# Reading x back in small packets and turning it on VectorE in a fused attention and FFN kernel

## The chip, the core and the metric

The kernel runs on one core of a Trainium2 chip. The time is device microseconds of one launch, the median of three runs; a profiled execution of the same program gives the trace. TensorE is the matrix engine, VectorE and ScalarE work on rows of up to 128 partitions, GpSimd (POOL) takes some elementwise work, and SP issues nearly all DMAs.

## The reference

Attention of 8 heads over 8 batches of 576 tokens, the first four heads local (each token sees the 32 up to itself), the last four strided (each sees the earlier ones at the same place modulo 32); then a layer norm, a two-layer FFN and the residual, all in float32:

```python
scores = scale * np.matmul(q, k.transpose(0, 1, 3, 2))        # q, k, v: (8, 8, 576, 64)
scores = np.where(masks, scores, -1e9)                        # local for h < 4, else strided
attn = softmax(scores)
x = np.matmul(attn, v).transpose(0, 2, 1, 3).reshape(8, 576, 512)
xn = (x - mean(x)) / sqrt(var(x) + 1e-6) * g_ln
out = x + np.maximum(xn @ w_ch1, 0.0) @ w_ch2                 # 512 -> 2048 -> 512
```

## The kernel before

**The FFN** runs in nine chunks of 512 tokens: chunk c below 8 is the first 512 tokens of batch c, chunk 8 the last 64 of all batches. A chunk has 16 steps, one for each 128 columns of the hidden layer. In a step, `ffn1` (L708 and L715) multiplies the step's part of w_ch1 by x, whose features stand on the partitions, into one PSUM tile `ph`; `h_high` (L720, ScalarE) and `h_low` (L725, VectorE) take the relu out of it in a high and a low part; `second` (L735) then does the second matrix for the step before. Each product is three matmuls with high and low parts, so x is needed as `xh` and `xl`, both with features on partitions and tokens on columns. The layer norm is folded in: w_ch1 is centred and scaled beforehand, and the row's scale is applied at the end (`finish`, L741) together with the residual. `ph` has a single buffer, so the next step's L708 waits for L720 and L725.

**The attention** of a batch is four pairs of heads, `Pair`, strided and local in turn. Batches 0 and 1, all weights and chunk 0 are ordered by hand in `ORDER`. From chunk 1 on the pairs of the batch behind the chunk's own are spread over the steps: the generator `pieces` (L893) takes one pair in four steps, called at L923 behind a step's relu and ahead of `second`. So chunks 1 to 6 hold the 24 pairs of batches 2 to 7. A pair is done as follows, `nxt` being the pair behind it:

- Step one, `m_piece`: TensorE makes the scores of `nxt` (L443) and the products of this pair with v (L514) in a PSUM tile; VectorE sums, masks and divides (L534 to L564) into `xo`; `v_store` (L576, L577 or L581) writes `xo` to a scratch tensor in DRAM, `xdl` for local pairs in the order of the tokens, `xds` for strided ones with the 32 residues outermost. Then the loads of v for two pairs on (L392, L393, L399).
- Step two: VectorE turns the raw q and k of the third pair on in 32x32 blocks (L413, L414, L418), and SP loads those of the fourth on (L349), 32 partitions by 18 groups of 128 bytes a DMA, eight DMAs. The raw tile has one buffer.
- Step three, `n_piece`: TensorE turns `xo` in 128x128 tiles (`x_turns`, L586; 4 for a local pair, 6 for a strided one) and the softmax numerators of `nxt` (`p_turn`, L499; 5 or 6), into one PSUM tile; ScalarE copies x out as `xh` (L613), VectorE subtracts for `xl` (L617), and ScalarE copies the turned numerators to `pt` (L504).
- Step four: nothing.

Near the end of a chunk, `x_load` (L671, L673) reads its rows of x back from the scratch for the residual, into tiles of the pool `tkp` (seven buffers), and `x_scale` (L678 to L683) takes their statistics; `finish` stores the output (L744, in the last chunk L747 as well).

The order of every engine's instructions, SP's included, is that of the program: a closing loop chains each instruction to the one before it on its engine. An instruction that waits holds up what stands behind it on its engine.

Of the kernel before, what the change touches and what calls it, by code (L numbers as in the profile page):

```python
# [8 lines left out]
F32 = mybir.dt.float32  # L9
# [55 lines left out]
def kernel(  # L65
# [10 lines left out]
    nc = tc.nc  # L76
# [3 lines left out]
    P = 128  # L80
    STR = 32
    NB = S // STR
    NG = (STR + 2) // 3
    GS = 3 * NB
    D1 = D + 1
    NL = (NB + 3) // 4
    NS = (NG + 1) // 2
    NCC = DM // P
    NFC = DFF // P
    CH = 512  # L90
# [10 lines left out]
    tkp = ctx.enter_context(tc.tile_pool(name="tkp", bufs=7))  # L101
# [31 lines left out]
    for jj in range(4):  # L133
        mrow = mask_l[STR * jj:STR * (jj + 1)]
        nc.gpsimd.affine_select(
            out=mrow, in_=mrow, pattern=[[1, 64]], base=-1,
            channel_multiplier=-1, compare_op=ALU.is_ge, fill=FILL)
        nc.gpsimd.affine_select(
            out=mrow, in_=mrow, pattern=[[-1, 64]], base=STR,
# [5 lines left out]
    for c in range(2):  # L145
        for r in range(3):
            msk = mask_s[64 * c:64 * (c + 1), NB * r:NB * (r + 1)]
            nc.gpsimd.affine_select(
                out=msk, in_=msk, pattern=[[-1, NB]], base=-NB * r,
                channel_multiplier=1, compare_op=ALU.is_ge, fill=FILL)  # L150
            nc.gpsimd.affine_select(
                out=msk, in_=msk, pattern=[[0, NB]], base=NB * r + NB - 1,
# [56 lines left out]
    xd_l = [dram.tile([S, DM // 2], F32, name=f"xdl{b}") for b in range(B)]  # L209
    xd_s = [dram.tile([2 * NS * GS, DM // 2], F32, name=f"xds{b}") for b in range(B)]  # L210
# [93 lines left out]
    def bank(name):  # L304
        pool, tag, n = banks[n_bank[0] % len(banks)]
        n_bank[0] += 1
        return pool.tile([P, n], F32, tag=tag, name=name)
# [11 lines left out]
    class Pair:  # L319
# [180 lines left out]

        def p_copy(self, pp):
            pool, tag = (early, f"pt{self.k % 2}") if self.b == 0 else (smp, "pt")
            self.pt = pool.tile([P, NS, P], F32, tag=tag, name=f"pt{self.id}")
            nc.scalar.copy(  # L504
                out=self.pt[:, 0:self.nt].rearrange("p t x -> p (t x)"), in_=pp[:, 0:P * self.nt])

        def v_block(self, n, h, at, w):
            if self.local:
                t, jj = divmod(n, 4)
                rows, cols = slice(64 * h, 64 * h + 64), slice(STR * jj, STR * (jj + 1))  # L510
            else:
                t, c = divmod(n, 2)
                rows, cols = slice(64 * h, 64 * h + GS), slice(64 * c, 64 * c + 64)
            nc.tensor.matmul(  # L514
                at(h, t)[cols], self.pt[rows, t, cols], self.v[rows, n, 0:w],
                start=True, stop=True, tile_position=(64 * h, cols.start))

        def v_full(self, ps):
            self.av = halves(ps, self.nt, D1)
# [36 lines left out]
        def v_divide(self, parts):  # L556
            nt = self.nt
            den = dens[self.i_den]
            if self.b == 0:
                xo = early.tile([P, NS, 2, D], F32, name=f"xo{self.id}")  # L560
            else:
                xo = xo_c
            for r, h0, h1, t0, t1, av in parts:
                nc.vector.tensor_tensor(  # L564
                    out=xo[r, t0:t1, h0:h1].rearrange("p t h d -> p h t d"), in0=av,
                    in1=den[r, h0:h1, t0:t1].unsqueeze(3).broadcast_to(
                        [r.stop, h1 - h0, t1 - t0, D]),
                    op=ALU.mult)
            self.xov = xo.rearrange("p t h d -> p t (h d)")

        def v_store(self):
            n0, nt, xov = self.n0, self.nt, self.xov
            cs = slice(P * n0, P * (n0 + 1))
            if self.local:
                x_b = xd_l[self.b]
                nc.sync.dma_start(x_b[0:CH, cs].rearrange("(t p) c -> p t c", p=P), xov[:, 0:NT])  # L576
                nc.sync.dma_start(x_b[CH:S, cs], xov[0:REST, NT])  # L577
            else:
                x_b = xd_s[self.b].rearrange("(t c s) d -> c s t d", c=2, s=GS)
                for c in range(2):  # L580
                    nc.sync.dma_start(x_b[c, :, :, cs], xov[64 * c:64 * c + GS, 0:nt])  # L581

        def x_turns(self, px):
            nt = NT if self.local else NS
            for t in range(nt):
                nc.tensor.transpose(px[:, P * t:P * (t + 1)], self.xov[:, t], ident)  # L586
            return nt
# [32 lines left out]
    def m_piece(p, nxt):  # L620

        ps = bank(f"m{p.id}")
        parts = nxt.s_blocks(ps) if nxt else None
        p.v_sums()
        av = p.v_blocks(ps)
        if nxt:
            nxt.s_masked(parts)
        p.v_divide(av)
        p.v_store()
        if nxt:  # L630
            nxt.s_sub()
            nxt.s_exp()

    def n_piece(p, nxt):

        ps = bank(f"n{p.id}")
        n = P * p.x_turns(ps)
        if nxt:
            nxt.p_turn(ps[:, n:])
        p.x_high(ps)  # L640
        p.x_low()
        if nxt:
            nxt.p_copy(ps[:, n:])

    def split_x(hi, lo, src):
        nc.scalar.activation(out=hi, in_=src, func=AF.Copy)
        nc.vector.tensor_tensor(out=lo, in0=src, in1=hi.bitcast(F32), op=ALU.subtract)
# [3 lines left out]
    def x_t(c):  # L651
        if c not in xt:
            xt[c] = tuple(xtp.tile([P, NCC, CH], F32R, tag=t, name=f"{t}{c}")
                          for t in ("xh", "xl"))
        return xt[c]
# [4 lines left out]
    pairs = [Pair(b, hp) for b in range(B) for hp in order]  # L660
# [62 lines left out]
    def h_low(c, f, ph, hh):  # L723
        hl = hp_.tile([P, CH], F32R, tag="hl", name=f"hl{c}_{f}")
        nc.vector.scalar_tensor_tensor(  # L725
            out=hl, in0=ph, scalar=0.0, in1=hh.bitcast(F32), op0=ALU.max, op1=ALU.subtract)
        return hl
# [53 lines left out]
    ps, ph, hs, splits = {}, {}, {}, {}  # L781
# [111 lines left out]
    def pieces():  # L893
        for i in range(2 * NHP, NP):
            nxt = pairs[i + 1] if i + 1 < NP else None
            m_piece(pairs[i], nxt)
            if i + 2 < NP:
                pairs[i + 2].load_v()
            yield
            if i + 3 < NP:  # L900
                pairs[i + 3].t_piece()
            if i + 4 < NP:
                pairs[i + 4].load_qk()
            yield
            n_piece(pairs[i], nxt)
            yield
            yield

    gen = pieces()
    ps_r_ctx.close()  # L910
    ps_m = ctx.enter_context(tc.tile_pool(name="ps_m", bufs=1, space=bass.MemoryType.PSUM))
    banks[:] = [(ps_m, "m", 1536)]

    for c in range(1, NCHUNK):
        xres = []
        tail = {}
        for f in range(NFC):
            ph = ffn1(c, f)
            hh = h_high(c, f, ph)
            h = hh, h_low(c, f, ph, hh)  # L920
# [3 lines left out]
            elif c + 1 == B:  # L924
                i = f // 2 - 1
# [6 lines left out]
            i = f - (NFC - NT - 3)  # L932
# [49 lines left out]
```

## Time and profile before

| | us |
|---|---|
| median of 3 runs (933.94 to 936.65) | 936.09 |
| the profiled execution | 935.35 |
| its span, first to last instruction | 933.5 |
| TensorE matmuls busy (7852) | 915.0 |
| TensorE weight loads busy, beside the matmuls | 756.8 |
| VectorE busy | 407.2 |
| ScalarE busy | 222.6 |
| GpSimd busy | 148.1 |

The mean granted clock of TensorE over the span is 0.992 of full speed. Matmul records overlap, as the next one starts before the end of the one before; where the time per instruction matters, it is read from the distance of starts in the timeline. The trace of DMAs has their issue on SP and the share of the span in which the 16 DMA engines are busy, but no landing of a single DMA.

### The profile page before, as it was taken

What the parts mean: (1) busy time and instruction counts of PE and PEld (TensorE: products, weight loads), DVE (VectorE), ACT (ScalarE), POOL (GpSimd) and SP (SyncE); (2) the same over time, 40 slices, a digit from 0 to 9 for tenths busy, and PEclk for the clock granted to TensorE, in tenths of its full rate; (3) what the DMA queues carried; (4) which work ended last, traced back from release to release, by engine and by line L of the source; (5) the groups of instructions that cost most, each with busy time, mean ns of one, the idle gap of its engine ahead of it and who ended that gap; (6) DMA issues with size and microseconds to landing.
All of it is one profiled execution on the core that took longest, in us unless ns stands there. A gap on an engine that the chain in (4) does not pass through costs nothing.

```text
span 933.5 us, 18590 instructions
## 1 busy us (share of the span) xinstructions
PE 915.0 (98%) x7852; PEld 756.8 (81%) x7852; DVE 407.2 (44%) x829; ACT 222.6 (24%) x361; POOL 148.1 (16%) x186
## 2 busy tenths in 40 slices
PE   8699999999999999999999999999999999999997
PEld 7578888888888888888888888888888888888886
DVE  3878877333444454435443454334533321122112
ACT  4567662112111211111121211121211111111110
POOL 5568773000100010001000110001000000000000
PEclk9799999999999999999999999999999999999999
DMA  8987966333443344324342334334221130002001
GB/s 154 231 248 188 270 145 126 94 57 87 75 98 65 86 75 98 64 55 90 76 79 46 82 60 99 64 87 75 73 38 49 37 108 17 1 1 90 1 1 46
DMA packets 239459, 80.16 MB, mean 86 GB/s; under 512 B 190096, under 2 KB 232720, under 8 KB 239376
## 3 DMA queue, kind: packets, MB, share of 16 engines
q1 hardware_dynamic: 236672, 77.27, 36.3%
q10 hardware_dynamic: 2704, 1.70, 0.8%
q8 instruction: 62, 1.02, 0.5%
q14 instruction: 21, 0.17, 0.1%
HBM read 59.48 MB, written 19.46 MB: 85 GB/s over the span
## 4 chain that ended last, share of the span: by engine, by line
PE 89%; SPq 4%; DMA 3%; DVE 1%; issue 1%; POOL 0%; ACT 0%; DVEq 0%; ACTq 0%
PE po L735 40%; PE ph L708 26%; PE ph L715 13%; SPq L349 3%; PE m L514 2%; PE m L443 2%; PE n L499 1%; PE n L586 1%; DMA s<-in_moe_w_ch_dram 1%; PE t L369 1%; DMA rows<-in_q_dram 1%; DMA xds<-xo 1%; SPq L399 1%; PE s L443 1%; PE av L514 0%
## 5 line engine op out<-in xcount | busy, mean ns | idle before, releaser
L735 PE MATMUL po<-w,hh 128*128 128x512 f32 x1152 | 361.5, 395 | 0.0
L725 DVE SCALAR_TENSOR_TENSOR hl<-ph,hh 128x512 fp32r<-128x512 f32 x144 | 99.6, 692 | 459.7 <-ACT hh L720 459.2
L735 PEld LDWEIGHTS po<-w,hh 128*128 128x128 f32 x1152 | 211.7, 188 | 43.6
L708 PE MATMUL ph<-xh,w 128*128 128x512 f32 x576 | 225.9, 392 | 1.1 <-ACT w L292 0.9
L735 PE MATMUL po<-w,hl 128*128 128x512 f32 x576 | 225.0, 391 | 0.0
L708 PE MATMUL ph<-xl,w 128*128 128x512 f32 x576 | 224.3, 389 | 0.0
L720 ACT ACTIVATE hh<-ph 128x512 fp32r<-128x512 f32 x144 | 86.1, 598 | 500.7 <-PE ph L715 500.7
L715 PE MATMUL ph<-xh,w 128*128 128x512 f32 x576 | 154.6, 390 | 0.0
L708 PEld LDWEIGHTS ph<-xh,w 128*128 128x128 f32 x576 | 108.3, 188 | 23.8 <-ACT w L292 1.1
L735 PEld LDWEIGHTS po<-w,hl 128*128 128x128 f32 x576 | 108.1, 188 | 23.2
L708 PEld LDWEIGHTS ph<-xl,w 128*128 128x128 f32 x576 | 108.3, 188 | 22.0
L715 PEld LDWEIGHTS ph<-xh,w 128*128 128x128 f32 x576 | 107.7, 188 | 22.3
L489 POOL TENSOR_TENSOR sm<-sm,mx 128x648 f32<-128x648 f32 (+1 forms) x32 | 40.7, 1271 | 404.4 <-DVE mx L484 404.4
L683 POOL TENSOR_TENSOR rs<-rs,mhalf 128x1 f32<-128x1 f32 x36 | 19.8, 550 | 340.3 <-DVE rs L682 340.3
L495 ACT ACTIVATE sm<-sm 128x648 f32<-128x648 f32 (+1 forms) x32 | 23.8, 744 | 118.1 <-POOL sm L489 118.1
L296 POOL TENSOR_TENSOR w<-r,w 128x512 fp32r<-128x512 f32 x32 | 41.0, 1297 | 9.1 <-ACT w L292 8.7
L617 DVE TENSOR_TENSOR xl<-n,xh 128x480 fp32r<-128x480 f32 (+2 forms) x36 | 22.7, 662 | 15.5 <-ACT xh L613 15.5
L484 DVE TENSOR_REDUCE mx<-sm 128x12 f32<-128x648 f32 (+1 forms) x32 | 26.3, 823 | 2.1
L564 DVE TENSOR_TENSOR xo<-m,den 64x64 f32<-64x64 f32 (+3 forms) x120 | 27.1, 290 | 0.1
L741 DVE SCALAR_TENSOR_TENSOR x<-po,rs,x 128x512 f32<-128x512 f32 x36 | 24.5, 739 | 3.1 <-PE po L735 2.8
L678 DVE BATCH_NORM_STATS2 st<-x 128x6 f32<-128x512 f32 x36 | 24.3, 675 | 0.0
L613 ACT ACTIVATE xh<-n 128x480 fp32r<-128x480 f32 (+2 forms) x36 | 20.7, 649 | 11.3 <-PE n L499 11.3
(98 smaller groups left out, 611.0 us busy)
## 6 DMA issues: line engine op xcount, KB each, us to landing
s<-in_moe_w_ch_dram SPq DMA_DIRECT2D x32, 512.0 KB
out_dram<-x SPq DMA_DIRECT2D x32, 256.0 KB
raw<-in_q_dram SPq DMA_DIRECT2D x112, 72.0 KB
raw<-in_k_dram SPq DMA_DIRECT2D x112, 72.0 KB
xds<-xo SPq DMA_DIRECT2D x32, 162.0 KB
v_l<-in_v_dram SPq DMA_DIRECT2D x32, 144.0 KB
xdl<-xo SPq DMA_DIRECT2D x16, 256.0 KB
x<-xdl SPq DMA_DIRECT2D x32, 128.0 KB
```

The lines of the kernel that those rows point to most:

```text
L296: nc.gpsimd.tensor_tensor(out=t[:, 1], in0=self.w[i], in1=t[:, 0].bitcast(F32), op=ALU.subtract)
L349: nc.sync.dma_start(self.raw[p0:p0 + 32, i].rearrange("p (g e) -> p g e", e=32), src[self.b, self.h0 + h].rearrange("(g t) d -> t g d", t=32)[
L443: nc.tensor.matmul(o, lhsT, rhs, start=True, stop=True, tile_position=(64 * h, pos))
L484: nc.vector.reduce_max(mx[:, :, 0:nt], sm, axis=AX.X)
L489: nc.gpsimd.tensor_tensor(out=sm, in0=sm, in1=mx[:, :, 0:nt].unsqueeze(3).broadcast_to([P, 2, nt, sm.shape[3]]), op=ALU.subtract)
L564: nc.vector.tensor_tensor(out=xo[r, t0:t1, h0:h1].rearrange("p t h d -> p h t d"), in0=av, in1=den[r, h0:h1, t0:t1].unsqueeze(3).broadcast_to(
L708: nc.tensor.matmul(ph, w1h[:, cc], x[:, cc, :], start=(new and n == 0 and i == 0), stop=False)
L715: nc.tensor.matmul(ph, w1l[:, cc], xt[c][0][:, cc, :], start=False, stop=(cc == NCC - 1))
L720: nc.scalar.activation(out=hh, in_=ph, func=AF.Relu)
L725: nc.vector.scalar_tensor_tensor(out=hl, in0=ph, scalar=0.0, in1=hh.bitcast(F32), op0=ALU.max, op1=ALU.subtract)
L735: nc.tensor.matmul(po[i], hx[:, cs], w, start=(f == 0 and n == 0), stop=(f == NFC - 1 and n == 2))
L741: nc.vector.scalar_tensor_tensor(out=x, in0=po[i], scalar=rs, in1=x, op0=ALU.mult, op1=ALU.add)
```

## The change

For the 24 pairs of `pieces`, x is no longer turned by TensorE out of `xo`. Right behind the store, `x_raw` reads the pair's 512 tokens of 128 features back from the scratch with four DMAs, each for 32 features: token t of a group of 32 goes to partition t, so every packet is 32 floats, 128 bytes, at a row pitch of 1 KB in DRAM. In step three `x_blocks` turns that tile in 32x32 blocks on VectorE, into the space of `xo`, which the store has left by then, and splits the result into `xh` and `xl` by one ScalarE copy and one VectorE subtraction (`split_x`), for both kinds of pairs. The numerators of the next pair are turned by TensorE as before, in a PSUM tile of their own, and copied to `pt` ahead of the split. Batches 0 and 1 are as before.

```diff
+        def x_raw(self):
+            self.xraw = tkp.tile([P, CH], F32, tag="tk", name=f"xraw{self.id}")
+            x_b = (xd_l if self.local else xd_s)[self.b]
+            for j in range(4):
+                c0 = P * self.n0 + 32 * j
+                cols = x_b[:, c0:c0 + 32]
+                src = (cols[0:CH].rearrange("(g t) e -> t g e", t=32) if self.local else
+                       cols[0:STR * NB].rearrange("(t g) e -> t g e", g=NB)[:, 0:CH // 32, :])
+                nc.sync.dma_start(
+                    self.xraw[32 * j:32 * j + 32].rearrange("p (g e) -> p g e", e=32), src)
+
+        def x_blocks(self):
+            xh, xl = x_t(self.b)
+            cc = self.h0 // 2
+            xT = self.xo.rearrange("p t h d -> p (t h d)")[:, 0:CH]
+            nc.vector.transpose(xT, self.xraw)
+            split_x(xh[:, cc, :], xl[:, cc, :], xT)
...
-    def n_piece(p, nxt):
-
-        ps = bank(f"n{p.id}")
-        n = P * p.x_turns(ps)
-        if nxt:
-            nxt.p_turn(ps[:, n:])
-        p.x_high(ps)
-        p.x_low()
-        if nxt:
-            nxt.p_copy(ps[:, n:])
...
             m_piece(pairs[i], nxt)
+            pairs[i].x_raw()
             if i + 2 < NP:
                 pairs[i + 2].load_v()
             yield
@@
-            n_piece(pairs[i], nxt)
+            if nxt:
+                pp = bank(f"pp{nxt.id}")
+                nxt.p_turn(pp)
+                nxt.p_copy(pp)
+            pairs[i].x_blocks()
             yield
             yield
```

The rest of the diff lets `v_block` fetch the numerators' columns through a function that `p_copy` sets, with the same operands as before, and keeps a reference to `xo`.

## Rows read from the trace of the kernel before

**Rows 1.** The page's totals: busy us (share of the span) and instructions of each engine.

```profile
PE 915.0 (98%) x7852; PEld 756.8 (81%) x7852; DVE 407.2 (44%) x829; ACT 222.6 (24%) x361; POOL 148.1 (16%) x186
```

**Rows 2.** The page's chain of work that ended last, as shares of the span: by engine, then by line.

```profile
PE 89%; SPq 4%; DMA 3%; DVE 1%; issue 1%; POOL 0%; ACT 0%; DVEq 0%; ACTq 0%
PE po L735 40%; PE ph L708 26%; PE ph L715 13%; SPq L349 3%; PE m L514 2%; PE m L443 2%; PE n L499 1%; PE n L586 1%; DMA s<-in_moe_w_ch_dram 1%; PE t L369 1%; DMA rows<-in_q_dram 1%; DMA xds<-xo 1%; SPq L399 1%; PE s L443 1%; PE av L514 0%
```

**Rows 3.** Groups of instructions by line and shape over the whole span, TensorE's matmuls (transposes are matmuls with the identity): count, then busy us, mean ns of one, then idle us in front of them and what ended it.

```profile
L735 PE MATMUL po<-w,hh 128*128 128x512 f32 x1152 | 361.5, 395 | 0.0
L708 PE MATMUL ph<-xh,w 128*128 128x512 f32 x576 | 225.9, 392 | 1.1 <-ACT w L292 0.9 <-DMA s<-in_moe_w_ch_dram 0.3
...
L499 PE MATMUL n<-ident,sm 128*128 128x128 f32 x126 | 17.5, 273 | 0.0
...
L586 PE MATMUL n<-ident,xo 128*128 128x128 f32 x120 | 17.0, 272 | 0.0
```

**Rows 4.** TensorE's timeline in chunk 3 and 4: start us, length us, line, output and inputs, count. A turning step of a local pair from 441.01, a step without turns from 447.57, a turning step of a strided pair from 465.87, and the first matmul of the step behind the next.

```profile
441.01 1.07 PE L715 MATMUL ph<-xh,w 128*128 128x512 f32 x4
441.92 0.60 PE L586 MATMUL n<-ident,xo 128*128 128x128 f32 x4
442.35 0.82 PE L499 MATMUL n<-ident,sm 128*128 128x128 f32 x6
...
445.76 0.39 PE L708 MATMUL ph<-xh,w 128*128 128x512 f32 x1
...
447.57 1.07 PE L715 MATMUL ph<-xh,w 128*128 128x512 f32 x4
...
451.20 0.39 PE L708 MATMUL ph<-xh,w 128*128 128x512 f32 x1
...
465.87 1.07 PE L715 MATMUL ph<-xh,w 128*128 128x512 f32 x4
466.78 0.82 PE L586 MATMUL n<-ident,xo 128*128 128x128 f32 x6
467.43 0.71 PE L499 MATMUL n<-ident,sm 128*128 128x128 f32 x5
...
470.73 0.39 PE L708 MATMUL ph<-xh,w 128*128 128x512 f32 x1
...
476.17 0.39 PE L708 MATMUL ph<-xh,w 128*128 128x512 f32 x1
```

**Rows 5.** TensorE's timeline in chunk 0, where the turns of x and those of the numerators stand apart.

```profile
131.20 0.82 PE L586 MATMUL px<-ident,xo 128*128 128x128 f32 x6
131.77 0.47 PE L708 MATMUL ph<-xh,w 128*128 128x512 f32 x1
132.08 0.39 PE L708 MATMUL ph<-xl,w 128*128 128x512 f32 x1
...
137.64 0.71 PE L499 MATMUL pp<-ident,sm 128*128 128x128 f32 x5
138.11 0.48 PE L708 MATMUL ph<-xh,w 128*128 128x512 f32 x1
```

**Rows 6.** VectorE's timeline in the same stretch as rows 4: start us, length us, line, operation, output and inputs, count, in brackets its idle time before.

```profile
462.83 0.77 DVE L413 STREAM_TRANSPOSE qt_l<-raw 128x576 f32<-128x576 f32 x1
...
467.66 0.69 DVE L725 SCALAR_TENSOR_TENSOR hl<-ph,hh 128x512 fp32r<-128x512 f32 x1 [3.40 <-ACT hh L720]
...
474.34 0.69 DVE L725 SCALAR_TENSOR_TENSOR hl<-ph,hh 128x512 fp32r<-128x512 f32 x1 [3.81 <-ACT hh L720]
...
487.81 1.25 DVE L418 STREAM_TRANSPOSE qt_s<-raw 128x576 f32<-128x576 f32 x1
...
499.21 0.69 DVE L725 SCALAR_TENSOR_TENSOR hl<-ph,hh 128x512 fp32r<-128x512 f32 x1 [4.84 <-ACT hh L720]
```

**Rows 7.** Groups of instructions by line and shape over the whole span, columns as in rows 3: the statistics of x, the split of x of a local pair.

```profile
L678 DVE BATCH_NORM_STATS2 st<-x 128x6 f32<-128x512 f32 x36 | 24.3, 675 | 0.0
...
L617 DVE TENSOR_TENSOR xl<-n,xh 128x512 fp32r<-128x512 f32 x12 | 8.3, 691 | 3.8 <-ACT xh L613 3.8
...
L613 ACT ACTIVATE xh<-n 128x512 fp32r<-128x512 f32 x12 | 7.2, 601 | 4.8 <-PE n L499 4.8
```

**Rows 8.** SP's timeline in the same stretch: start us, length us of the issues, line, destination and source, count.

```profile
440.33 2.77 SPq L349 DMA_DIRECT2D raw<-in_q_dram  x4
443.14 2.54 SPq L349 DMA_DIRECT2D raw<-in_k_dram  x4
459.57 0.72 SPq L581 DMA_DIRECT2D xds<-xo  x2
...
468.73 2.12 SPq L349 DMA_DIRECT2D raw<-in_k_dram  x4
...
484.69 0.50 SPq L577 DMA_DIRECT2D xdl<-xo  x1
```

**Rows 9.** Two stretches: length us, busy us (instructions) of TensorE, its weight loads, VectorE, ScalarE and GpSimd, then the granted clock, the busy share of the DMA engines and GB/s.

```profile
440.30:447.00 6.70, 6.70 (x36) 5.66 (x35) 3.14 (x9) 2.00 (x3) 1.10 (x2) 1.00 0.64 115
929.60:932.00 2.40, 0.00 (x0) 0.00 (x0) 0.00 (x0) 0.00 (x0) 0.00 (x0) 0.99 0.85 289
```

**Rows 10.** SP's timeline at the end of the kernel, the last output stores.

```profile
927.17 2.47 SPq L747 DMA_DIRECT2D out_dram<-x  x4
```

**Rows 11.** The chain that ended last, in order of time, in the start of the kernel: start us, length us, what.

```profile
47.37 0.36 SPq L399
...
47.77 3.27 DMA v_s<-in_v_dram
```

More of the change, by code (lines that the diff above doesn't have):

```diff
@@ L502, in p_copy @@
             pool, tag = (early, f"pt{self.k % 2}") if self.b == 0 else (smp, "pt")
-            self.pt = pool.tile([P, NS, P], F32, tag=tag, name=f"pt{self.id}")
+            pt = pool.tile([P, NS, P], F32, tag=tag, name=f"pt{self.id}")
             nc.scalar.copy(
-                out=self.pt[:, 0:self.nt].rearrange("p t x -> p (t x)"), in_=pp[:, 0:P * self.nt])
+                out=pt[:, 0:self.nt].rearrange("p t x -> p (t x)"), in_=pp[:, 0:P * self.nt])
+            w = STR if self.local else 64
+            self.p_cols = lambda rows, t, j: pt[rows, t, w * j:w * (j + 1)]
         def v_block(self, n, h, at, w):
[L508 to L513, printed above, removed]
+            t, j = divmod(n, 4 if self.local else 2)
+            k, m = (64, STR) if self.local else (GS, 64)
+            rows = slice(64 * h, 64 * h + k)
             nc.tensor.matmul(
-                at(h, t)[cols], self.pt[rows, t, cols], self.v[rows, n, 0:w],
-                start=True, stop=True, tile_position=(64 * h, cols.start))
+                at(h, t)[m * j:m * (j + 1)], self.p_cols(rows, t, j), self.v[rows, n, 0:w],
+                start=True, stop=True, tile_position=(64 * h, m * j))
         def v_full(self, ps):
@@ L568, in v_divide @@
                     op=ALU.mult)
+            self.xo = xo
             self.xov = xo.rearrange("p t h d -> p t (h d)")
```

## The prediction

> **What bounds the kernel now.** I read the totals first: TensorE is busy for 915.0 of 933.5 us, VectorE for 44% of the span [rows 1]. Then the chain of work that ended last: 89% of it is TensorE's, and two of its lines are the turns in question, L586 and L499 of TensorE [rows 2]. Then the idle time in front of the FFN's matmuls: none but 1.1 us in all [rows 3]. So from chunk 0's end to the last chunk TensorE runs from one instruction to the next, at a granted clock of 1.00 where I looked [rows 9], and a TensorE instruction taken out there shortens the kernel by its own length, as long as nothing makes TensorE wait in its place. The profiled execution took 935.35 us, its span 933.5; the 1.85 us around it don't change. It stands 0.74 us under the median of 936.09.
>
> **What is removed from TensorE.** Line 586 turned x of each pair of heads in six batches: 120 transposes [rows 3], 4 for a local pair and 6 for a strided one, 12 pairs of each. One lasts 272 ns in the records, but they overlap, so I take the distance of their starts instead. In a local pair the four begin at 441.92 and the next group at 442.35: 0.43 us, 0.108 each. In a strided pair six begin at 466.78 and the next group at 467.43: 0.65 us, 0.108 each [rows 4]. 120 x 0.108 = 13.0 us. From below: in chunk 0, where turns of one sort stand alone, six take 131.20 to 131.77, 0.095 each [rows 5], so 11.4 us. From above: in a local turning step 445.76 - 441.01 = 4.75 us pass from L715 to the next step's L708, in a step without turns 451.20 - 447.57 = 3.63 (sixteen matmuls, 0.23 each) [rows 4], 1.12 more for ten turns. Six turns alone cost 0.57 and slow the next matmul by 0.08 (0.31 instead of 0.23 to the one behind it) [rows 5], 0.65, so four save 0.47. In a strided step it is 470.73 - 465.87 = 4.86, 1.23 more for eleven; five alone cost 0.47 + 0.08 [rows 5], so six save 0.68. 12 x (0.47 + 0.68) = 13.8 us. I take 13.0, the distance in the very steps that change. The turns of the numerators (L499) and the slower first matmul behind them stay.
>
> **What is added on VectorE and ScalarE.** Per pair one turn of 128x512 in 32x32 blocks on VectorE. The nearest row turns 128x576 in 0.77 us [rows 6], an upper bound for eight ninths of the columns; 24 x 0.77 = 18.5 us in all. The copy on ScalarE (0.60) and the subtraction on VectorE (0.69) are those that a local pair has already [rows 7]; a strided pair loses its longer ones in two parts for them. They now read an on-chip tile and not PSUM, which no row shows for this form; by the other 128x512 operations of the two engines 0.6 to 0.75. All of it lies in the step's shadow: after L725, the last of a step's relu, which ends at 468.35, VectorE is next wanted at 474.34 [rows 6], 6.0 us later, 5.3 once the step is 0.65 shorter. The new work is 0.77 + 0.60 + 0.69 and an estimated 0.1 for the handovers, 2.16 us. At a chunk's end the statistics of x (0.68 and two small ones [rows 7]) stand there too and still fit. Without that cover the work would delay L725, and with it the reuse of the one PSUM tile of the first FFN matrix: L725 ends at 475.03 and TensorE writes that tile again at 476.17 [rows 4, 6], so a further 1.14 us are free before TensorE waits.
>
> One page of the Trainium skill speaks against the change: "VectorE: DVE Perf Modes", Rules for kernel authors, sends a 128x128 transpose to TensorE if PSUM will do as its place. By durations alone the rows bear the page out: 0.77 us on VectorE [rows 6] against 0.43 for four turns on TensorE [rows 4]. But by the totals the engine with time to spare is VectorE [rows 1]; what it costs if that is untrue is the fourth rival.
>
> **What is added on SP and the DMA engines.** Per pair four DMAs of 64 KB in packets of 128 bytes, 2048 packets, issued right behind the store of the divided rows and waiting for that store, as they read what it writes. The nearest row is the load of q and k, eight DMAs of 576 such packets, issued from 440.33 to 445.68 [rows 8]. Between 440.3 and 447.0 the DMA engines are busy for 0.64 of 6.7 us [rows 9]: 4.29 x 16 / 4608 = 14.9 ns a packet. So 2048 packets are 1.9 us of the 16 engines, less than their issue, 2.12 to 2.77 us for four [rows 8].
>
> The landing is put together from four parts. The store's end: no row shows it by itself; at the kernel's end the stores of the output are issued until 927.17 + 2.47 = 929.64 [rows 10], bytes move until 932.0 [rows 9], and the span ends at 933.5, so 2.4 to 3.9 us after the last issue. Then the issue, 2.12 to 2.77. Then from the last issue to the landing: 445.68 to 447.0, 1.3 us, from below; 3.27 us in the chain, of a load of v in the crowded start, from above [rows 11]. Together 5.8 to 9.9 us after the store's issue. For a strided pair that ended at 460.29 [rows 8]: landed between 466.1 and 470.2. Landing before 468.35, when VectorE gets to it, has no effect at all; landing until 474.34 + 1.14 - 0.65 - 2.16 = 472.7 has none on TensorE. A local pair, stored by 485.19 [rows 8], lands between 491.0 and 495.1; the next L725 is at 499.21 [rows 6], so the limit is 499.21 + 1.14 - 0.43 - 2.16 = 497.8. In both some 2.5 us are left over the upper bound, so I cost the wait at nothing.
>
> **What stands behind the wait on SP.** SP stops for the store's end and issues four more DMAs: 4.5 to 6.7 us per pair. Behind it are the loads of v (wanted two pairs, some 49 us, later), at a chunk's start the output stores, and the loads of q and k. Where most is queued, the latter now end their issue at 470.85 [rows 8]; 6.7 later is 477.6, landed by 480.8 with the 3.27 from above; VectorE turns them at 487.81 [rows 6]. Cost nothing, with 6 us to spare. The copy of the turned numerators on ScalarE moves ahead of the split of x and has its own PSUM tile; its reader is two steps away. The tile for the read-back comes from the pool of seven that the residual rows use; four residual tiles and two read-backs are alive at most.
>
> The sum: -13.0 + 0 + 0, so 935.35 to 922.3 for the profiled execution, **923.1 us** for the median.
>
> **The rivals.**
> 1. The forecast holds: 936.09 - 13.0 = 923.1 (922.3 to 924.7 by the two bounds, and 1.5 us either way for the spread of the runs shown). Chance 0.74.
> 2. Part of it is lost to new short waits: SP's longer queue or the pool of tiles makes some of the read-backs late. A quarter of a microsecond of TensorE's time per pair is 24 x 0.25 = 6 us: 929. Against it stands the margin above; for it, that the landing is put together from other transfers. Chance 0.12.
> 3. Slower than before: the read-back lands late in every pair. VectorE and ScalarE both stand at the turn, the next step's relu is held up, the PSUM tile isn't free, and TensorE waits. In the strided pair that costs from 472.7 on and has eaten the whole gain (13.0 / 24 = 0.54 us) at 473.2, 12.9 us after the store was issued. With the store's slow end (3.9 us) and 0.5 us for the first issue that asks for 66 ns a packet, 4.4 times the 14.9 of the rows. One microsecond beyond the limit gives 923.1 + 24 = 947. For it speaks that the reads go to rows of 1 KB pitch just written, which those of q and k do not. Chance 0.07. The page "DMA: Bandwidth & Descriptors", Specifications, of the Trainium skill wants 512 bytes for full rate; the small packets of q and k agree (115 GB/s at 0.64 busy, against 289 at 0.85 at the end [rows 9]).
> 4. VectorE's turn is on the path: 24 x 0.77 - 13.0 = 5.5 us are lost, 941.6. It needs VectorE to be wanted within 2.2 us of L725, and the rows show 6.0 [rows 6]. Chance 0.02. This is how the rule on transposes quoted above would come out.
> 5. TensorE's freed time turns into a wait that exists already and is hidden, for the relu for instance: 936. The steps without turns are shorter than the changed ones will be, and no idle time stands in front of their matmuls [rows 3, 4]. Chance 0.05.
>
> **How the numbers follow.** About 0.3% (2.8 us) is what a measurement of this kernel can tell from no change. Faster: cases 1 and 2, 0.86; within it: case 5, 0.05; slower: 3 and 4, 0.09. The range goes from 920.5 (the bound of 13.8 and the spread) to 931 (most of case 2), and leaves out some 0.17.
>
> **What would show it.** Right: no L586 behind chunk 0, TensorE's turning step shorter by 0.4 and 0.65 us, no idle time in front of L708, VectorE's wait for the read-back zero or under 2 us. Wrong: idle time of TensorE released by ScalarE or VectorE, VectorE's turn waiting for the DMA beyond 4 us, or SP's loads of q and k reaching into the next pair's turn.

## The result and the profile after

The changed kernel takes 920.02 us (median of 4 runs, 919.72 to 923.3) against 935.39 of the kernel before on the same chip (median of 4, 933.94 to 936.65): ratio 0.9844, 95% interval 0.9817 to 0.9872. Run again beside two of the experiments it took 922.00 against 933.59, 0.9876 (0.9861 to 0.9891). So the two measurements gain 15.4 and 11.6 us where 13.0 were forecast. Its profiled execution took 920.26 us, its span 918.4.

The page's totals of the changed kernel answer to [rows 1], and its chain, by engine and by line, to [rows 2]:

```profile
PE 900.8 (98%) x7732; PEld 742.5 (81%) x7732; DVE 417.2 (45%) x841; ACT 215.8 (23%) x349; POOL 147.7 (16%) x186
...
PE 92%; DMA 3%; DVE 2%; issue 1%; SPq 1%; ACT 0%; DVEq 0%; POOL 0%; ACTq 0%
PE po L744 42%; PE ph L717 28%; PE ph L724 14%; PE m L513 2%; PE m L443 2%; PE pp L499 2%; DMA s<-in_moe_w_ch_dram 1%; DMA rows<-in_q_dram 1%; PE t L369 1%; PE s L443 1%; SPq L349 0%; PE px L606 0%; PE av L513 0%; PE cm L279 0%; DVE xo L563 0%
```

TensorE lost 120 matmuls and 14.2 us of busy time and is as full as before, 98%. The turns of x are gone from the chain but for those of chunk 0 (L606 now). L708, L715, L725 and L735 of before are L717, L724, L734 and L744 here. The group of L717, over the whole span, answers to [rows 3]:

```profile
L717 PE MATMUL ph<-xh,w 128*128 128x512 f32 x576 | 226.2, 393 | 1.8 <-ACT w L292 1.6
```

Of the 1.8 us of idle time in front of it 1.6 are waits for the preparation of the weights (L292), in the start; from chunk 1 on the view of waits has none of a matmul.

TensorE's timeline of the changed kernel, the turning step of a strided pair from 457.23 and of a local pair from 481.57, answers to [rows 4]:

```profile
457.23 1.08 PE L724 MATMUL ph<-xh,w 128*128 128x512 f32 x4
458.15 0.71 PE L499 MATMUL pp<-ident,sm 128*128 128x128 f32 x5
...
461.45 0.39 PE L717 MATMUL ph<-xh,w 128*128 128x512 f32 x1
...
481.57 1.08 PE L724 MATMUL ph<-xh,w 128*128 128x512 f32 x4
482.48 0.82 PE L499 MATMUL pp<-ident,sm 128*128 128x128 f32 x6
...
485.87 0.39 PE L717 MATMUL ph<-xh,w 128*128 128x512 f32 x1
```

The strided step lasts 461.45 - 457.23 = 4.22 us instead of 4.86, the local one 485.87 - 481.57 = 4.30 instead of 4.75: 0.64 and 0.45 us shorter. That is 0.107 and 0.112 us for each of the six and four turns taken out.

SP's timeline of the changed kernel in the same stretch answers to [rows 8], the stores of a strided and a local pair and what follows them:

```profile
450.94 0.72 SPq L581 DMA_DIRECT2D xds<-xo  x2
454.72 1.90 SPq L592 DMA_DIRECT2D xraw<-xds  x4
...
464.34 2.12 SPq L349 DMA_DIRECT2D raw<-in_k_dram  x4
474.92 0.39 SPq L576 DMA_DIRECT2D xdl<-xo  x1
475.41 0.51 SPq L577 DMA_DIRECT2D xdl<-xo  x1
477.31 1.90 SPq L592 DMA_DIRECT2D xraw<-xdl  x4
```

SP stands still from 451.66 to 454.72, 3.06 us, until the strided store has landed, and from 475.92 to 477.31, 1.39 us, for the local one. Over the 24 pairs it is 3.02 to 3.19 us for strided stores and 1.39 to 1.47 for local ones. Four read-backs take 1.90 us to issue. VectorE's timeline of the same pairs, answering to [rows 6]:

```profile
459.04 0.69 DVE L734 SCALAR_TENSOR_TENSOR hl<-ph,hh 128x512 fp32r<-128x512 f32 x1 [3.14 <-ACT hh L729]
459.65 0.70 DVE L600 STREAM_TRANSPOSE xo<-xraw 128x512 f32<-128x512 f32 x1
461.05 0.69 DVE L656 TENSOR_TENSOR xl<-xo,xh 128x512 fp32r<-128x512 f32 x1 [0.70 <-ACT xh L655]
465.06 0.69 DVE L734 SCALAR_TENSOR_TENSOR hl<-ph,hh 128x512 fp32r<-128x512 f32 x1 [3.33 <-ACT hh L729]
```

The block turn follows the relu without a wait for the read-back, as in all 24 pairs, takes 0.70 us, and the split is through at 461.74, 3.3 us ahead of the next relu. One thing was not foreseen. Of the page of waits, who waited for whom in us, times and longest:

```profile
DVE st L687 <- DMA x<-xds: 21.1, 10, 3.9
```

VectorE's statistics of the residual rows (L687, L678 before) wait for their loads in ten places; in the kernel before they never waited [rows 7]. SP, held behind the stores, issues those loads later: in chunk 3 the first begins 12.8 us behind the end of the strided store's issue instead of 8.4. VectorE's timeline at the first of these waits in chunk 3 shows how near that comes to the next relu:

```profile
416.32 0.69 DVE L734 SCALAR_TENSOR_TENSOR hl<-ph,hh 128x512 fp32r<-128x512 f32 x1 [3.32 <-ACT hh L729]
420.90 0.69 DVE L687 BATCH_NORM_STATS2 st<-x 128x6 f32<-128x512 f32 x1 [3.89 <-DMA x<-xds]
...
421.91 0.68 DVE L734 SCALAR_TENSOR_TENSOR hl<-ph,hh 128x512 fp32r<-128x512 f32 x1
```

The relu at 421.91 has no idle time before it any more: it waited for the statistics and not for ScalarE.

**Where 15.1 us come from.** The span is 15.1 us shorter, but not all of it lies where something changed. The first scores of `pieces`, which open chunk 1, stand in TensorE's timeline at these places, in the kernel before:

```profile
154.97 0.97 PE L443 MATMUL m<-kt_l,qt_l 64*32 64x64 f32 x72
```

and in the changed one:

```profile
152.88 0.97 PE L443 MATMUL m<-kt_l,qt_l 64*32 64x64 f32 x72
```

Ahead of that place each engine has the same instructions in the same order in both. From there to the end (called the rest from here on) it is 933.5 - 154.97 = 778.5 us before and 918.4 - 152.88 = 765.5 after: 13.0 us. The other 2.1 lie in the start. In thirteen traces it lasts from 151.05 to 155.04 us, so 2.1 is within what one execution differs from another there. The table gives the rest for every run, each from one trace. It is the steadier measure: the two traces of the changed kernel differ by 1.4 us in the start and by 0.5 in the rest.

| run | chunk 1 begins | span | rest | time, ratio to before (95% interval) |
|---|---|---|---|---|
| before | 154.97 | 933.5 | 778.5 | |
| changed | 152.88 | 918.4 | 765.5 | 920.02, 0.9844 (0.9817 to 0.9872) |
| e1, turns of x on TensorE kept as well | 155.04 | 933.2 | 778.2 | 933.43, 1.0001 (0.9983 to 1.0018) |
| e2, no read-back | 153.18 | 919.0 | 765.8 | 920.67, 0.9859 (0.9834 to 0.9884) |
| e3, read-back doubled | 151.47 | 922.3 | 770.8 | 925.14, 0.9912 (0.9884 to 0.9940) |
| e4, turn in step one | 152.36 | 1110.3 | 957.9 | 1112.97, 1.1923 (1.1886 to 1.1960) |
| e5, residual rows ahead | 153.97 | 920.0 | 766.0 | 921.54, 0.9875 (0.9856 to 0.9895) |
| e6, both of e3 and e5 | 152.43 | 918.7 | 766.3 | 920.94, 0.9876 (0.9852 to 0.9900) |
| e7, local pairs only | 153.03 | 926.7 | 773.7 | 928.66, 0.9950 (0.9931 to 0.9969) |
| e8, strided pairs only | 152.29 | 923.4 | 771.1 | 927.92, 0.9950 (0.9930 to 0.9970) |
| e9, turn in step two | 151.05 | 918.7 | 767.7 | 921.59, 0.9879 (0.9856 to 0.9903) |
| e10, last chunk by blocks too | 153.76 | 917.7 | 763.9 | 919.68, 0.9850 (0.9827 to 0.9874) |
| e11, changed again | 154.29 | 920.3 | 766.0 | 922.00, 0.9876 (0.9861 to 0.9891) |

### The profile page after: what moved, and what is told of

Read it like the earlier page. It is cut to its first block, busy times and chain, and to the rows that moved or that the text cites. A ratio compares the mean times of both kernels' runs of the same rounds, so it can differ in the third digit from the quotient of the medians.

```text
span 918.4 us, 18465 instructions
## 1 busy us (share of the span) xinstructions
PE 900.8 (98%) x7732; PEld 742.5 (81%) x7732; DVE 417.2 (45%) x841; ACT 215.8 (23%) x349; POOL 147.7 (16%) x186
## 4 chain that ended last, share of the span: by engine, by line
PE 92%; DMA 3%; DVE 2%; issue 1%; SPq 1%; ACT 0%; DVEq 0%; POOL 0%; ACTq 0%
PE po L744 42%; PE ph L717 28%; PE ph L724 14%; PE m L513 2%; PE m L443 2%; PE pp L499 2%; DMA s<-in_moe_w_ch_dram 1%; DMA rows<-in_q_dram 1%; PE t L369 1%; PE s L443 1%; SPq L349 0%; PE px L606 0%; PE av L513 0%; PE cm L279 0%; DVE xo L563 0%
## 5 line engine op out<-in xcount | busy, mean ns | idle before, releaser
L744 PE MATMUL po<-w,hh 128*128 128x512 f32 x1152 | 361.4, 395 | 0.0
L734 DVE SCALAR_TENSOR_TENSOR hl<-ph,hh 128x512 fp32r<-128x512 f32 x144 | 99.6, 691 | 413.6 <-ACT hh L729 413.3
L744 PEld LDWEIGHTS po<-w,hh 128*128 128x128 f32 x1152 | 211.7, 188 | 43.6
L717 PE MATMUL ph<-xh,w 128*128 128x512 f32 x576 | 226.2, 393 | 1.8 <-ACT w L292 1.6
L717 PE MATMUL ph<-xl,w 128*128 128x512 f32 x576 | 224.9, 390 | 0.0
L744 PE MATMUL po<-w,hl 128*128 128x512 f32 x576 | 224.9, 390 | 0.0
L724 PE MATMUL ph<-xh,w 128*128 128x512 f32 x576 | 154.8, 390 | 0.0
L717 PEld LDWEIGHTS ph<-xh,w 128*128 128x128 f32 x576 | 108.4, 188 | 24.6 <-ACT w L292 1.8
L744 PEld LDWEIGHTS po<-w,hl 128*128 128x128 f32 x576 | 108.1, 188 | 23.1
L717 PEld LDWEIGHTS ph<-xl,w 128*128 128x128 f32 x576 | 108.4, 188 | 22.1
L724 PEld LDWEIGHTS ph<-xh,w 128*128 128x128 f32 x576 | 107.7, 188 | 22.3
L687 DVE BATCH_NORM_STATS2 st<-x 128x6 f32<-128x512 f32 x36 | 24.4, 677 | 21.1 <-DMA x<-xds 21.1
L504 ACT COPY pt<-pp 128x768 f32<-128x768 f32 (+1 forms) x32 | 23.9, 746 | 11.6 <-PE pp L499 11.6
L499 PE MATMUL pp<-ident,sm 128*128 128x128 f32 x176 | 26.0, 284 | 0.5 <-ACT sm L495 0.5
```

What stands on the lines that cost most here:

```text
L499: nc.tensor.transpose(pp[:, P * t:P * (t + 1)], self.sm[:, t].rearrange("p h x -> p (h x)"), ident)
L717: nc.tensor.matmul(ph, w1h[:, cc], x[:, cc, :], start=(new and n == 0 and i == 0), stop=False)
L724: nc.tensor.matmul(ph, w1l[:, cc], xt[c][0][:, cc, :], start=False, stop=(cc == NCC - 1))
L734: nc.vector.scalar_tensor_tensor(out=hl, in0=ph, scalar=0.0, in1=hh.bitcast(F32), op0=ALU.max, op1=ALU.subtract)
L744: nc.tensor.matmul(po[i], hx[:, cs], w, start=(f == 0 and n == 0), stop=(f == NFC - 1 and n == 2))
```

## The experiments

The theory: the time falls by TensorE's own time of the removed turns, and everything added lies in cover, that is, in time for which TensorE does not wait. The rivals: part of the gain comes from elsewhere or is fixed for each piece; the read-back costs something already; the cover is wide and nothing is near a limit.

**e1: the removed turns put back, all else left as changed.**

```diff
                 pp = bank(f"pp{nxt.id}")
-                nxt.p_turn(pp)
-                nxt.p_copy(pp)
+                n = P * pairs[i].x_turns(pp)
+                nxt.p_turn(pp[:, n:])
+                nxt.p_copy(pp[:, n:])
             pairs[i].x_blocks()
```

> The changed kernel with the 120 turns of x kept on TensorE as well; their result is written to PSUM and not used, everything else (store, read-back, turn on VectorE, split) is as in the changed kernel. Theory (the gain is TensorE's own time of the turns, and the read-back costs nothing): 13.0 us more than the changed kernel, 933 us, about 0.3% under the kernel before at most. Rival (part of the gain came from elsewhere, such as the shorter ScalarE and VectorE work of a strided pair or the earlier copy of the numerators): clearly under 930.

933.43 us, ratio 1.0001, and a rest of 778.2 against 778.5: with the turns back on TensorE the whole gain is gone (12.7 us of the 13.0 by the rests), and the wait for the store, the four DMAs, the block turn and the new split cost nothing beside them. The rival falls.

**e2: the read-back taken away.**

```diff
-            x_b = (xd_l if self.local else xd_s)[self.b]
-            for j in range(4):
...
-                nc.sync.dma_start(
-                    self.xraw[32 * j:32 * j + 32].rearrange("p (g e) -> p g e", e=32), src)
+            nc.gpsimd.memset(self.xraw, 0.5)
```

> The changed kernel without the read-back: the tile is filled with a constant by GpSimd, so x of batches 2 to 7 is a constant in the first FFN matrix; store, turn on VectorE and split stay. Theory: 920 us within 1.5, as the read-back is hidden, and VectorE's waits for the residual rows (21.1 us in 10 waits in the changed kernel) are gone, as nothing holds SP behind the store. Rival (the read-back still costs something in some pairs): 917 or less.

920.67 us, rest 765.8 against 765.5 and 766.0 of the two traces of the changed kernel: the read-back costs no time. VectorE has no wait for residual rows in this trace, so those waits come from the read-back: from SP's wait for the store, its four issues or the transfers, which this run takes away together.

**e3: the read-back doubled.** Eight DMAs a pair into two tiles, of which the second is used.

```diff
-            self.xraw = tkp.tile([P, CH], F32, tag="tk", name=f"xraw{self.id}")
-            for j in range(4):
+            for j in range(8):
+                if j % 4 == 0:
+                    self.xraw = tkp.tile([P, CH], F32, tag="tk", name=f"xraw{self.id}_{j}")
+                j = j % 4
```

> The changed kernel with every read-back done twice, into two tiles, the second one used: eight DMAs a pair instead of four. Theory with the margins as forecast: the used tile lands some 2.0 us later, still inside the margin, so no pair pays for it by itself; but the residual rows behind it on SP come 2 us later too, VectorE's statistics in step 11 then end some 2.3 us behind the place of the next relu, 1.1 us more than is free, so about 1.1 us a chunk in six chunks: 926 (922 to 930). Rival 1 (nothing is near a limit): 920. Rival 2 (the read-back itself is at its limit): 24 pairs pay 1 us or more each, 944 or more.

925.14 us, the rest 5.3 us longer than in the first trace of the changed kernel and 4.8 longer than in the second: the size expected, but TensorE pays at another place than expected. From the view of waits, of VectorE and of TensorE:

```profile
DVE st L689 <- DMA x<-xds: 43.7, 10, 5.5
...
DVE xo L602 <- DMA xraw<-xds: 12.6, 12, 1.6
...
PEld ph L719 <- DVE hl L736: 5.5, 5, 1.8
...
PE ph L719 <- DVE hl L736: 3.3, 4, 1.4
```

VectorE waits some 1 us for each strided read-back, and no such wait stands ahead of one of TensorE's; three short ones for local read-backs do (1.6 us together), but VectorE waits for a residual tile behind them all the same. The four idle times of TensorE's matmuls (at 247.34, 346.62, 444.97 and 641.17) follow the statistics of the fourth residual tile. VectorE's timeline ahead of the longest of them, and TensorE's behind it:

```profile
344.87 0.69 DVE L689 BATCH_NORM_STATS2 st<-x 128x6 f32<-128x512 f32 x1 [4.05 <-DMA x<-xds]
...
345.89 0.68 DVE L736 SCALAR_TENSOR_TENSOR hl<-ph,hh 128x512 fp32r<-128x512 f32 x1
```

```profile
346.62 0.50 PE L719 MATMUL ph<-xh,w 128*128 128x512 f32 x1 [1.37 <-DVE hl L736]
```

The longer wait, 5.5 us for the first tile in step 11, delays no matmul where it stands: TensorE does the scores and products of the next pair in step 12 before it wants the PSUM tile again. Behind the fourth tile's statistics in step 14 stands the relu of step 15, a step without attention work for TensorE, and there a wait of 4.05 us is too long. By the distance of starts, as the turns were priced, the four places cost 1.3, 1.6, 0.7 and 0.8 us, 4.4 of the 5.3 (or 4.8) that are lost. Why the fourth tile is that late is seen beside e6.

**e5 and e6: the residual rows ahead of the read-back,** in the changed kernel and in e3.

```diff
+        rows = []
         for f in range(NFC):
+            if c + 1 < B and f == 8:
+                rows += [x_load(c, i) for i in range(3)]
...
-                xres.append([x_load(c, i)])
+                xres.append([rows[i] if i < len(rows) else x_load(c, i)])
```

> The changed kernel with the first three residual tiles of a chunk loaded ahead of step 8's pair, so ahead of its read-back on SP, in chunks 1 to 6. Theory: the waits of VectorE's statistics for the residual rows (21.1 us in 10) nearly vanish, TensorE has nothing from it, 920 us within 1.5. Rival (those waits already cost TensorE something): 917 or less.

> The doubled read-back together with the residual rows loaded ahead. Theory (what the doubled read-back costs, it costs through the residual rows behind it on SP): 920 to 921, and VectorE's waits for residual rows gone. Rival (the doubled read-back costs by its own landing): as slow as the doubled read-back alone.

e5: 921.54 us, rest 766.0; VectorE's waits for residual rows fall from 21.1 us to 5.8, in the five places of the fourth tile, and the rest is that of the second trace of the changed kernel. So the waits cost it nothing. e6: 920.94 us, rest 766.3 against 770.8 of e3. The waits for the fourth tile are 16.6 us in five places, 3.6 the longest, those for the read-back 13.9, and no matmul of TensorE waits behind them. What the doubled read-back costs, it costs through the residual rows behind it on SP.

Only the first three tiles are loaded earlier here; the load of the fourth stands behind the doubled read-back as in e3, and yet it costs nothing. So the loss of e3 begins at the first tile. The relu of step 11, which the first tile's statistics follow, and the last issue of the local pair's store in step 12, in chunk 2 of e3 and of e6:

```profile
318.84 0.69 DVE L736 SCALAR_TENSOR_TENSOR hl<-ph,hh 128x512 fp32r<-128x512 f32 x1 [1.80 <-ACT hh L731]
...
330.99 0.50 SPq L577 DMA_DIRECT2D xdl<-xo  x1
```

```profile
318.51 0.69 DVE L736 SCALAR_TENSOR_TENSOR hl<-ph,hh 128x512 fp32r<-128x512 f32 x1 [1.31 <-ACT hh L731]
...
328.93 0.51 SPq L577 DMA_DIRECT2D xdl<-xo  x1
```

In e6 the store is issued 10.93 us behind the relu, in e3 12.65, as VectorE stood waiting for the first tile before it divided the rows that are stored. The read-back and the fourth tile stand behind that store on SP. Over chunks 1 to 5 the store of e3 is 1.17, 1.72, 0.72, 0.52 and 1.00 us later than in e6, and TensorE's matmuls are idle for 1.00, 1.37, 0.42, nothing and 0.50 us: the delay reaches TensorE, less 0.2 to 0.5 us.

**e4: the turn and split in step one.**

```diff
             pairs[i].x_raw()
+            pairs[i].x_blocks()
...
                 nxt.p_copy(pp)
-            pairs[i].x_blocks()
```

> The changed kernel with the turn and split in step one, right behind the read-back's issue, instead of step three. Theory (VectorE and ScalarE stand at the turn until the read-back has landed, and the next relu and the PSUM tile wait behind them): a local pair lands about 5 us behind its store, which delays TensorE by some 3.4 us, a strided one about 6.3 us behind it, 5.2 us, and 8 us where the chunk's output also stands behind it on VectorE; 20 us a chunk, 120 in all, 1040 us (1015 to 1065), and TensorE's idle time is released by ScalarE or VectorE. Rival (the engines' wait is absorbed elsewhere): under 960.

1112.97 us, above the range of 1015 to 1065. The mechanism is the one expected, the price 193 us instead of 120. This run shows what the trace of before had no row for, the landing: VectorE does nothing but wait for it. SP's and VectorE's timelines for a local and a strided pair:

```profile
452.64 0.51 SPq L577 DMA_DIRECT2D xdl<-xo  x1
455.15 1.91 SPq L592 DMA_DIRECT2D xraw<-xdl  x4
...
483.88 0.72 SPq L581 DMA_DIRECT2D xds<-xo  x2
487.70 1.90 SPq L592 DMA_DIRECT2D xraw<-xds  x4
```

```profile
458.81 0.71 DVE L600 STREAM_TRANSPOSE xo<-xraw 128x512 f32<-128x512 f32 x1 [6.56 <-DMA xraw<-xdl]
...
491.29 0.71 DVE L600 STREAM_TRANSPOSE xo<-xraw 128x512 f32<-128x512 f32 x1 [7.43 <-DMA xraw<-xds]
```

From the last issue to the turn: 458.81 - 457.06 = 1.75 us and 491.29 - 489.60 = 1.69. From the store's issue to the turn: 458.81 - 453.15 = 5.66 us for this local pair, 491.29 - 484.60 = 6.69 for the strided one. The local pair shown is the slowest of its kind, as SP waits 2.00 us for its store; the other eleven take 4.96 to 5.22 us. The strided ones take 6.59 to 6.96. TensorE's waits in this run:

```profile
PE ph L717 <- DVE hl L734: 84.5, 18, 5.7
PE po L744 <- DVE x L750: 54.4, 6, 9.2
```

138.9 us in all, one wait for each of the 24 pairs; the six with the chunk's output behind the turn are the longest. That is 19 more than forecast. What else is lost is not idle time. Stretches of 5 us, length, busy time and count of TensorE, its weight loads, VectorE, ScalarE, GpSimd, then granted clock, DMA share and GB/s:

```profile
455.00:460.00 5.00, 2.20 (x10) 1.50 (x8) 0.71 (x1) 0.44 (x1) 0.00 (x0) 0.97 0.72 126
460.00:465.00 5.00, 3.44 (x8) 2.76 (x9) 3.54 (x4) 0.67 (x2) 0.00 (x0) 0.50 0.39 49
465.00:470.00 5.00, 5.00 (x23) 4.05 (x23) 0.69 (x1) 1.39 (x2) 0.00 (x0) 0.85 0.69 112
```

TensorE's timeline ahead of the wait in these stretches and behind it:

```profile
452.73 0.39 PE L717 MATMUL ph<-xl,w 128*128 128x512 f32 x1
452.96 0.39 PE L717 MATMUL ph<-xh,w 128*128 128x512 f32 x1
...
461.56 0.79 PE L717 MATMUL ph<-xh,w 128*128 128x512 f32 x1 [4.37 <-DVE hl L734]
462.16 0.63 PE L717 MATMUL ph<-xl,w 128*128 128x512 f32 x1
462.58 0.63 PE L717 MATMUL ph<-xh,w 128*128 128x512 f32 x1
```

During a wait of 4.4 us the granted clock falls to 0.50 of full speed, 1.2 GHz; behind it the starts of the matmuls lie 0.43 us apart instead of 0.23, and the clock is back at 2.4 GHz within the next stretch. Over the span the granted clock is 0.921 instead of 0.990. 53 us of the loss are not idle time (1110.3 - 918.4 - 138.9). The trace has 24 stretches at 0.50 from chunk 1 on, one at each of the 24 waits, and TensorE is busy for 100.2 us in them. At the full clock's distance of starts the same work would take some 54 us, so by this estimate the clock accounts for 47 of the 53; the last 6 are not separated.

**e9: the turn and split in step two,** between e4 and the changed kernel.

```diff
                 pairs[i + 4].load_qk()
+            pairs[i].x_blocks()
             yield
...
-            pairs[i].x_blocks()
```

> The changed kernel with the turn and split in step two, behind the turns of the raw q and k, one step earlier than in the changed kernel and one later than in the run that had them in step one. With the landing that the run with step one showed (1.7 us behind the last issue): a strided pair waits on VectorE for about 2.4 us, ends its split about 60.4 - 59.0 = 1.4 us behind the place of the next relu's start, and the PSUM tile is free some 0.3 us before TensorE wants it; a local pair hardly waits. Theory: 920 us within 1.5, with about 12 x 2.4 = 29 us of waits of VectorE for the read-back in the trace. Rival (any wait of VectorE is passed on to TensorE, as in step one): 935 or more.

921.59 us, beside 922.00 of the changed kernel in the same set of runs. The waits:

```profile
DVE xo L600 <- DMA xraw<-xds: 31.3, 10, 4.5
...
DVE xo L600 <- DMA xraw<-xdl: 4.9, 3, 2.4
...
PE ph L717 <- DVE hl L734: 1.3, 2, 0.8
```

36 us of waits on VectorE, and 5.9 more at two strided pairs, which the view puts down to the load of v behind the read-back; 37 us of the 42 are strided pairs', where 29 were expected. TensorE's matmuls wait for 1.3 us; the rest is 1.7 to 2.2 us longer than in the two traces of the changed kernel. VectorE's timeline at the strided read-back of chunk 4, and at the first of the two places where TensorE waits, with TensorE's line of that place:

```profile
457.68 0.71 DVE L600 STREAM_TRANSPOSE xo<-xraw 128x512 f32<-128x512 f32 x1 [2.44 <-DMA xraw<-xds]
...
311.66 0.71 DVE L600 STREAM_TRANSPOSE xo<-xraw 128x512 f32<-128x512 f32 x1 [3.99 <-DMA xraw<-xds]
```

```profile
314.42 0.50 PE L717 MATMUL ph<-xh,w 128*128 128x512 f32 x1 [0.76 <-DVE hl L734]
```

The wait of 2.44 us delays no matmul, nor do those of up to 3.02 at eight other strided pairs, nor the 4.55 at the last one, which begins 1.4 us earlier as VectorE has no raw q and k left to turn there. Of 3.99 TensorE sees 0.76, and at the second place, of 3.77, 0.54. In both 3.23 us are free and what goes beyond is paid in full: by these two places the limit is sharp, and half a microsecond further out than expected (2.4 + 0.3).

**e7 and e8: local pairs only, strided pairs only.**

The `n_piece` of the kernel before is put back for the pairs that stay on TensorE. In e8 the condition is `not pairs[i].local`.

```diff
+            blocks = pairs[i].local
-            pairs[i].x_raw()
+            if blocks:
+                pairs[i].x_raw()
...
+            if blocks:
...
+                pairs[i].x_blocks()
+            else:
+                n_piece(pairs[i], nxt)
```

> Only the 12 local pairs of batches 2 to 7 go by the read-back (48 turns off TensorE), the strided ones by TensorE as before. Theory (0.108 us for each turn): 5.2 us under the kernel before, 930.2. Rival (a piece's gain is fixed, not by the number of turns): half of the whole gain, 6.5 to 7.5 us.

> Only the 12 strided pairs go by the read-back (72 turns off TensorE). Theory: 7.8 us under the kernel before, 927.6; together with the local ones alone the two gains make the whole one. Rival (fixed gain a pair): the same as the local ones.

The times can't tell the two apart: 928.66 and 927.92 against 933.52, both 0.9950, with intervals of 0.2% either way; by the medians 4.9 and 5.6 us, where 5.2 and 7.8 were forecast. The rests come nearer: 778.53 - 773.67 = 4.86 us for 48 turns and 778.53 - 771.11 = 7.42 for 72, 0.101 and 0.103 us for each, together 12.3 of the 13.0. A fixed gain of 6.5 for each kind is 0.9 to 1.6 us off, but two traces of one kernel already differ by 0.5. TensorE's timelines settle it. Read as in [rows 4], from the last four matmuls of the first matrix to the first of the next step, the turning step of a strided pair lasts 4.86 to 4.87 us in e7, as before, and 4.22 in e8; that of a local pair 4.31 to 4.33 in e7 and 4.75 in e8, as before. So a strided pair gives 0.64 us for six turns and a local one 0.43 for four, 0.11 a turn in both. The gain goes with the number of turns.

**e10 and e11: the last chunk's x the same way,** beside the changed kernel. In chunk 7 the loads of `xt` and the 16 turns of L699 give way to 128 small DMAs and four block turns.

```diff
-                i = f // 2 - 1
-                if f % 2 == 0 and i < NT:
-                    if i + 1 < NT:
-                        tail[i + 1] = x_load(B, i + 1, "xt")
-                    if i >= 0:
-                        x_turn(B, i, tail[i])
+                if f == 0:
+                    tail[7] = rest_raw(True)
+                elif f == 1:
+                    rows = [x_load(c, i) for i in range(NT)]
+                    tail[14] = rest_raw(False)
+                elif f in tail:
+                    rest_blocks(f == 7, tail[f])
...
-                xres.append([x_load(c, i)])
+                xres.append([rows[i] if c + 1 == B else x_load(c, i)])
```

`rest_raw` reads the 64 last tokens of each batch for 32 features at a time (local heads or strided ones); `rest_blocks` turns and splits two tiles.

> The changed kernel with the last chunk's x by the same way: in chunk 7, instead of four loads and 16 turns on TensorE, 128 small DMAs of 128-byte packets (64 for each kind of head), four block turns of 128x512 on VectorE, and the residual rows of chunk 7 loaded at its start. Theory: 16 x 0.108 = 1.7 us less than the changed kernel, 918.3, as SP and VectorE have time in that chunk. Rival (128 issues of half a microsecond, 64 us, run into the turns or the residual rows): 920 or more, with TensorE waiting in chunk 7 or 8.

> The changed kernel once more, on the same chip as the two runs sent with it, for comparison. 920 within 1.5; the start of chunk 1 (152.9 us in the first trace, 155.0 in that of the kernel before) anywhere between 151 and 156, as the instructions ahead of it are the same in both.

919.68 us against 922.00; their ratios to the kernel before, 0.9850 and 0.9876, have intervals that overlap. The rests are 763.9 against 765.5 and 766.0, 1.6 to 2.1 us less, which agrees with the 1.7 of the 16 turns. TensorE's matmuls wait nowhere from chunk 1 on, so the rival's waits are not there. It is the lowest rest of all, by a difference that the traces show and the times alone do not. The 922.00 of the changed kernel lies 0.5 above the 918.5 to 921.5 expected of e11, as e5 and e9 lie 0.04 and 0.09 above the same range.

## Why the prediction was right

**TensorE as the bound, and the turns as the term.** 13.0 us were forecast. The stretch that changed gives 13.0 and 12.5 by the two traces, the two kinds of step 12 x (0.64 + 0.45) = 13.1; e1 gives 12.7 back, and e7 and e8 gain in proportion to the turns. The distance of starts was the right price, between the two bounds; the 0.272 us of one record would have made 33 us of it. No matmul waits from chunk 1 on, and VectorE waits neither for the read-back nor for the raw q and k. That one trace gives just 13.0 is luck, by the 0.5 us between two traces. The median of 920.02 lies 3.1 us under the forecast 923.1 and 0.5 under the lower end of the range, 920.5: the kernel before took 935.39 beside it and not 936.09, and of the 15.1 us between the two traces 2.1 lie in the start, where nothing was changed. The ratio of 0.9844, taken from 936.09, gives 921.5.

**VectorE and ScalarE.** 2.16 us forecast for turn, copy and subtraction, 461.74 - 459.65 = 2.09 measured; reading the on-chip tile costs nearly what reading PSUM did (0.69 us for the subtraction, and 0.63 instead of 0.60 for the copy). One block turn takes 0.70 us, longer than the four or six turns on TensorE, and yet the kernel is faster without those, as e1 shows: what counts is which engine the end waits for. The rule of the Trainium skill that sends a 128x128 transpose to TensorE where PSUM will do, "VectorE: DVE Perf Modes", Rules for kernel authors, comes out the other way in this kernel.

**The landing.** 5.8 to 9.9 us forecast; 6.59 to 6.96 for strided pairs and 4.96 to 5.66 for local ones measured in e4. Of its parts the store lands in some 3.1 us (strided) or 1.4 (local) against 2.4 to 3.9, the issue takes 1.90 against 2.12 to 2.77, the landing some 1.7 against 1.3 to 3.3. So the local store and the issue lie below their bounds and the others inside, and the margin was larger than the forecast 2.5 us. In the changed kernel VectorE comes to a strided pair's turn about 8.0 us behind the store's issue, so by the landing of e4 the read-back is there 1.0 to 1.4 us before. e9, a step earlier, shows the limit for TensorE: 3.23 us of waiting are free there and the next are not. One reading in the forecast is a little high: the stretch of the 14.9 ns a packet holds 4903 packets by the view of DMAs, not only the 4608 of q and k, which makes 14.0.

**What stands behind the wait on SP.** Here the list was short of one: the loads of residual rows stand there too, and their reader on VectorE comes two steps later in the program whether they have landed or not. The wait on SP was forecast to cost nothing and does (e2, e5), but with less to spare than was thought: with 2 us more on SP for each pair the first tile's wait delays the next store, and TensorE pays some 4.4 us behind the fourth tile (e3, e6). For the raw q and k, which were on the list, 487.81 - 480.8 is 7.0 us and not 6.

**The price of the third rival.** "One microsecond beyond the limit" was put at 24 us. e9 bears it out for waits under a microsecond, 0.76 and 0.54 us paid where the landing lies that far beyond the limit. e4 bears out the mechanism and shows the price too low where the waits are long: 193 us are lost for 138.9 of waits, as the clock falls in them.

## What to carry to other kernels

Where one engine runs without a gap, price what is taken from it by the distance of starts in the very steps that change, and compare the stage that changed, not the whole span, if the start differs from run to run. A wait put on an in-order DMA queue is paid by whatever stands behind it: list every load behind it with its reader's place, the ones of other stages too. And a buffer written and read back through DRAM needs its landing measured once: put the reader directly behind it, read the wait, and place it by that.

## What was not expected of the hardware

The strided store, two DMAs of 162 KB, took 3.02 to 3.19 us to land in the changed kernel, the local one of 256 KB and 32 KB 1.39 to 1.47, and both write rows of 512 bytes. Around the strided store (451.0 to 454.7) the DMA engines move 96 GB/s, around the local one (475.3 to 477.3) 148; why, no run here tells. TensorE's granted clock fell to 0.50 in each of the 24 waits of 3.65 to 9.17 us in e4; where it waited for up to 1.37 us in e3 and 0.76 in e9, it stayed at 1.00. And the start of the kernel, up to chunk 1, differs by up to 4 us between executions with the same order of instructions. The granted clock differs there too (between 20 and 50 us it is 0.75 in e1, which has the longest start, and 0.89 in e9, which has the shortest), but e7 and e9 have the same 0.89 there, 1.00 from then on, and starts 2.0 us apart; the cause is open.
